# Sliding-window attention scores on six PSUM banks at a time, two of them shared by two row tiles in turn

## The chip, the cores and the metric

The kernel runs on one core of one Trainium2 chip, as one launch. The metric is the device time in microseconds (us), the median over runs. TensorE (PE in the profile) does the matmuls and transposes into PSUM, used as eight banks of 512 fp32 columns; ScalarE (ACT) does exponentials and GELU, VectorE (DVE) the copies and sums, GpSimd (POOL) masks and small arithmetic, and SyncE (SP) issues the transfers.

## The reference

Two layers, each an attention block A and an MLP block B with the same weights in both layers, on x of 2048 rows by 576 columns in bf16. Cut to what matters:

```python
def _A_ref(x, wqkv, wo):
    H = 32; Dh = D // H; W = 256                       # 32 heads of 18 columns
    q, k, v = split(x @ wqkv)
    scores = jnp.einsum("bhqd,bhkd->bhqk", q, k) * (Dh ** -0.5)
    mask = (idx[:, None] - idx[None, :] >= 0) & (idx[:, None] - idx[None, :] < W)
    p = _softmax(jnp.where(mask[None, None], scores, -1e9), axis=-1)
    return einsum("bhqk,bhkd->bhqd", p, v).reshape(B, S, D) @ wo

def _B_ref(x, w1, b1, w2, b2):                         # 576 -> 4608 -> 576
    return _gelu(_layernorm(x) @ w1 + b1) @ w2 + b2

for layer in range(2):
    x = x + _A_ref(_layernorm(x), A_wqkv, A_wo)
    x = x + _B_ref(_layernorm(x), B_w1, B_b1, B_w2, B_b2)
```

A row attends to itself and the 255 rows before it. In tiles of 128 rows, a block of keys meets three blocks of queries: its own (masked on the diagonal), the next (whole), and the one after (masked on the other side).

## The kernel before

**Tiles and chunks.** The 16 row tiles of a layer form four chunks of 512 rows, so there are eight chunks over both layers (`CH`, k = 0 to 7; k = 0 and 4 begin a layer). A head has 18 columns, padded to 32, so four heads stand in the four 32-row tiles of TensorE at once; eight groups g of four heads make the 32.

**Scores.** `units_of` (line 884) cuts a chunk's blocks into three units of 384 or 512 query columns per head; a part `(so, qo, nq, col)` is key block `so` against `nq` query blocks from `qo`, put at column `col`. `scores` (line 898) does one unit of one group as one burst on TensorE: for each part four matmuls, one per row tile j, each into a bank of its own (line 909). A burst takes two pairs of banks out of `SC = (0, 2, 4)`. ScalarE then takes the exponential of each pair in one activation (line 918), and POOL sets the masked triangles to zero in SBUF (line 939). `pv` (line 944) multiplies a group's three units by V, in four column tiles, into one bank (line 956), and VectorE transposes and normalises that (lines 967 to 977).

**Order within attention.** `E` (line 992) emits the groups of a chunk: three units per group, and the `pv` of a group behind the first unit of the next. `E0` (line 980) does this for the first three groups of chunk 0. `CUTS = (0, 3, 6, 8)` splits the eight groups of a chunk into three stages, between which the MLP of the chunk before it runs.

**Everything else on TensorE.** `qkv` (line 819) makes q, k and v; behind the first two chunks and in the MLP's first product (`G_part`, line 1051, matmul at line 1076) the array is used as two 64-row tiles which swap banks between two phases, the second phase waiting on TensorE's own semaphore (`own=True`). `mm2` (line 1099) is the MLP's second product and `tail` (line 1029) the output projection; both go through `quad` (line 779), either as one full matmul (line 781) or as four quarter column tiles (line 784), so that they can stand next to `pv` in the same tile shape. Their sums take banks from `FILL = (7, 6, 5, 4)`, the output of `pv` from `OUT`, the same four; `G_part` may take all eight. VectorE adds the sums to the residual (`resid`, line 1012).

**What sets the order.** Nothing is issued in the order of the program text. `Plan.add` records tasks with costs, priorities and banks; `Plan.schedule` (line 263) replays them by those costs, picks banks, and fixes the order on every engine and queue. A task's priority has a hand-set part and a `nudge` per stage from a table (line 480). `keep_warm` (line 249) puts filler matmuls (line 683) on TensorE where the plan leaves it idle for over 0.4 us in the first 140 us. `Sched.add` (line 65) turns reads and writes into waits on semaphores.

Of the kernel before, what the change touches and what calls it, by code (L numbers as in the profile page):

```python
# [186 lines left out]
class Plan:  # L187
# [75 lines left out]
    def schedule(self):  # L263
# [156 lines left out]
        for st, t in order:  # L420
            names = lambda rs: [n for r in rs for n in ([f"pb{b}" for b in r.banks()] if isinstance(r, Bank) else [r])]
            if t.plain:
                self.S.plain(t.eng, t.fn)
            else:
                self.S.add(t.eng, t.fn, names(t.reads), names(t.writes), dma=t.dma, ring=t.ring, own=t.own)
# [11 lines left out]
def build_kernel(nc, A_x, A_wqkv, A_wo, B_x, B_w1, B_b1, B_w2, B_b2, out):  # L437
# [19 lines left out]
    PVG = [()] * 8  # L457
    PVLAG = 1
# [21 lines left out]
    PL.nudge = {"": -230.72, "b": 275.87, "ea0.0": 68.12, "ea0.2": -36.73, "ea0.p0": 25.27, "ea0.p1": 8.39, "ea0.p2": 19.16,  # L480
# [835 lines left out]
```

## Time and profile before

| | |
|---|---|
| median of 2 runs | 865.9 us (865.78 to 866.03) |
| the profiled execution, its own time | 864.13 us |
| its span, first to last instruction | 862.3 us |
| TensorE clock granted, mean | 0.998 |
| TensorE instructions (matmuls) | 11578 |
| score matmuls, line 909 | 1408 |
| exponentials, line 918 | 384, 345.1 us busy |
| GELU, line 1086 (hT) | 276, 167.4 us busy |
| masks, line 939 | 368, 282.8 us busy |

The profile is of one execution, taken by the hardware profiler. A line such as `L909 PE MATMUL ps<-qT,kT` names the line of the kernel, the engine, the operation and the tiles written and read; `x448` is how many instructions the row holds. PE is TensorE's matmuls, PEld its weight loads, which run beside them. In a timeline the columns are the start in us, the time from there to the last end, and what ran; `[0.37 <-PE ps L840]` is idle time of that engine just before, and what ended it. Several matmuls in different row or column tiles start almost together, and a matmul's record reaches beyond the time in which the next can start.

### The profile page before, as it was taken

The numbers are of one execution on the slowest core, as the hardware profiler recorded it, in microseconds if no ns is written. First come the engines' busy times: TensorE is split into PE (matmuls) and PEld (weight loads), VectorE is DVE, ScalarE is ACT, GpSimd is POOL, SyncE is SP. The second block draws the span as 40 slices with busy tenths as digits, with TensorE's granted clock in tenths as the row PEclk, the third lists the DMA queues.
The fourth block names the chain that finished last, engine by engine and source line by source line (L and its number), as shares of the span: only waits on it lengthen the run. The fifth ranks groups of instructions, "written<-read, shape, count | busy, mean of one in ns | idle before, by whom it ended". The sixth has DMA issues, their size and how long they took to land.

```text
span 862.3 us, 26990 instructions
## 1 busy us (share of the span) xinstructions
PE 848.7 (98%) x11578; PEld 520.5 (60%) x11578; DVE 392.0 (45%) x934; ACT 593.2 (69%) x741; POOL 377.9 (44%) x560
## 2 busy tenths in 40 slices
PE   8899999999999999999999999999999999999998
PEld 6556556656556565565655655656556656656656
DVE  7689424655228542384424832655224434243012
ACT  4796788768667588573875876737787589771730
POOL 4687544465135653264421863425454276222100
PEclk9999999999999999999999999999999999999999
DMA  7887435351583615957359443673536953355320
GB/s 192 197 193 142 124 125 148 109 163 44 166 181 107 163 43 166 204 93 169 90 151 218 92 139 125 116 177 98 173 112 119 289 155 105 126 166 146 120 83 28
DMA packets 181862, 119.77 MB, mean 139 GB/s; under 512 B 107440, under 2 KB 181744, under 8 KB 181744
## 3 DMA queue, kind: packets, MB, share of 16 engines
q1 hardware_dynamic: 181744, 118.05, 53.7%
q8 instruction: 91, 1.49, 0.7%
q14 instruction: 27, 0.22, 0.1%
HBM read 90.10 MB, written 2.36 MB: 107 GB/s over the span
## 4 chain that ended last, share of the span: by engine, by line
PE 87%; DMA 4%; DVE 4%; ACT 2%; issue 2%; SPq 1%; POOL 1%; POOLq 0%; DVEq 0%; ACTq 0%
PE ps L1076 31%; PE ps L781 27%; PE ps L784 9%; PE ps L840 8%; PE ps L909 6%; PE ps L956 4%; ACT pT L918 2%; DMA xnTm<-xn 2%; PE ps L800 1%; DMA xnTa<-xn 1%; DVE x_res L1019 1%; DVE xn L721 1%; DVE st_all L696 1%; SPq L633 1%; DMA wqkv<-in_A_wqkv_dram 1%
## 5 line engine op out<-in xcount | busy, mean ns | idle before, releaser
L939 POOL TENSOR_SCALAR_AFFINE_SELECT pT<-pT 128x512 bf16<-128x512 bf16 (+1 forms) x368 | 282.8, 789 | 250.1 <-ACT pT L918 244.9
L918 ACT ACTIVATE pT<-ps 128x1024 bf16<-128x1024 f32 (+1 forms) x384 | 345.1, 974 | 58.0 <-PE ps L909 57.6
L1076 PE MATMUL ps<-xnTm,w_sb 64*128 64x512 bf16 x2592 | 290.5, 376 | 0.9 <-DVE x_res L1019 0.3
L1086 ACT ACTIVATE hT<-ps,b1col 128x512 bf16<-128x512 f32 x276 | 167.4, 687 | 173.9 <-PE ps L1076 173.4
L1076 PEld LDWEIGHTS ps<-xnTm,w_sb 64*128 64x128 bf16 x2592 | 128.8, 94 | 142.5 <-issue 6.4
L781 PE MATMUL ps<-w_sb,hT 128*128 128x288 bf16 x1506 | 201.1, 287 | 0.0
L1019 DVE TENSOR_TENSOR x_res<-ps,x_res 128x288 f32<-128x288 f32 x224 | 100.0, 450 | 188.2 <-PE ps L781 162.1
L781 PEld LDWEIGHTS ps<-w_sb,hT 128*128 128x128 bf16 x1506 | 139.9, 98 | 51.5 <-issue 15.6
L840 PE MATMUL ps<-wqkv,xnTa 64*128 64x288 bf16 x1296 | 91.7, 283 | 1.6 <-DVE x_res L1019 1.1
L967 DVE STREAM_TRANSPOSE oq<-ps 128x512 f32<-128x512 f32 x64 | 45.8, 716 | 98.9 <-PE ps L956 98.0
L784 PE MATMUL ps<-w_sb,hT 128*32 128x288 bf16 x2424 | 83.7, 287 | 0.1
L861 DVE CAST qn<-ps 128x288 bf16<-128x288 f32 x120 | 49.0, 450 | 76.4 <-PE ps L840 68.8
L840 PEld LDWEIGHTS ps<-wqkv,xnTa 64*128 64x128 bf16 x1296 | 61.3, 94 | 31.4 <-issue 2.7
L784 PEld LDWEIGHTS ps<-w_sb,hT 128*32 128x32 bf16 x2424 | 62.2, 97 | 13.6 <-issue 4.2
L909 PE MATMUL ps<-qT,kT 32*128 32x384 bf16 (+2 forms) x1216 | 64.1, 276 | 2.8 <-ACT pT L918 2.3
L696 DVE BATCH_NORM_STATS2 st_all<-x_res 128x6 f32<-128x288 f32 (+1 forms) x128 | 53.4, 442 | 6.7 <-DMA x_res<-in_A_x_dram 5.8
L709 POOL TENSOR_SCALAR vtmp<-mv_all 128x1 f32<-128x1 f32 (+1 forms) x43 | 8.8, 204 | 107.7 <-DVE mv_all L700 105.3
L848 DVE CAST vA<-ps 128x288 bf16<-128x288 f32 x64 | 26.5, 450 | 63.2 <-PE ps L840 59.5
L1092 POOL TENSOR_TENSOR x_res<-x_res,b2bc 128x576 f32<-128x576 f32 x32 | 40.2, 1275 | 32.8 <-ACT hT L1086 32.8
L956 PE MATMUL ps<-pT,vA 128*20 128x384 bf16 (+2 forms) x1408 | 50.5, 276 | 0.2 <-DVE qn L861 0.2
L909 PEld LDWEIGHTS ps<-qT,kT 32*128 32x128 bf16 x1216 | 19.4, 92 | 42.8 <-issue 26.3
L781 PE MATMUL ps<-wo_sb,attT 128*128 128x288 bf16 x320 | 42.1, 287 | 0.3 <-DVE qn L861 0.3
(56 smaller groups left out, 465.1 us busy)
## 6 DMA issues: line engine op xcount, KB each, us to landing
w_sb<-in_B_w_dram SPq DMA_DIRECT2D x46, 864.0 KB, 6.0
w_sb<-in_B_w_dram SPq DMA_DIRECT2D x48, 768.0 KB, 4.7
w_sb<-in_B_w_dram SPq DMA_DIRECT2D x96, 48.0 KB, 4.4
wqkv<-in_A_wqkv_dram SPq DMA_DIRECT2D x3, 576.0 KB, 5.6
x_res<-in_A_x_dram SPq DMA_DIRECT2D x3, 576.0 KB, 5.7
wqkv<-in_B_w_dram SPq DMA_DIRECT2D x2, 864.0 KB, 6.3
out_dram<-x_res SPq DMA_DIRECT2D x12, 144.0 KB, 2.0
wo_sb<-in_A_wo_dram SPq DMA_DIRECT2D x4, 144.0 KB, 2.6
```

Of the source, the lines that this page charges most:

```text
L696: add("dve", lambda e, i=i, s=s: e.bn_stats(st_all[:, t, i, :], s[:, t, i * HB:(i + 1) * HB]), reads=res, writes=[f"st{t}_{i}"], cost=0.37 ...
L781: return e.matmul(bank(b)[:, 0:HB], lhs, rhs, start=start, stop=stop, skip_group_check=True)
L784: ins = e.matmul(bank(b)[32 * j:32 * j + 32, 0:HB], lhs[:, 32 * j:32 * j + 32], rhs, start=start, stop=stop, tile_position=(0, 32 * j), sk ...
L840: ins = e.matmul(bank(bs[o])[:, 0:HB], xnTa[r:r + 64, c, i * 128:(i + 1) * 128], wqkv[r:r + 64, c, col:col + HB], start=(c == 4), stop=(ph ...
L861: add("dve", lambda e, b=bs[o], dst=dst: e.tensor_copy(dst, heads_of(bank(b))), reads=[bs[o]], writes=[f"qn{sl}h{o}"], cost=0.375, lat=0.1 ...
L909: ins = e.matmul(two(bs[j // 2])[:, j % 2, col:col + nq * 128], k_of(T0 + so)[0][32 * j:32 * j + 32, g, :], qs[32 * j:32 * j + 32, g, qo * ...
L918: add("act", lambda e, h2=h2: e.activation(pT[:, sl, 2 * h2:2 * h2 + 2, lo:hi], two(bs[h2])[:, :, lo:hi], ACT.Exp, scale=SCALE), reads=[bs ...
L939: add("pool", lambda e, ap=ap, pat=pat, sgn=sgn, kind=kind: e.affine_select(ap, ap, pattern=pat, compare_op=(ALU.is_ge if kind == "d" else ...
L956: ins = e.matmul(bank(bo)[32 * j:32 * j + VW, qo * 128:(qo + nq) * 128], vA[:, (T0 + so) % VS, 8 * j + g, :], pT[:, sl, j, col:col + nq * ...
L1019: add("dve", lambda e: e.tensor_tensor(x_res[:, t, sl], bank(b)[:, 0:HB], x_old[:, t, sl], ALU.add), reads=[b] + ([f"xin{t}"] if first els ...
L1076: ins = e.matmul(bank(bks[i])[:, 0:n], w1_sb[r:r + 64, sls[i], col:col + 128], xnTm[r:r + 64, k % 2, c, 0:n], start=(c == 4), stop=(ph == ...
L1086: add("act", lambda e, ff=ff, hd=hd, bk=bk: e.activation(hd[:, 0:n], bank(bk)[:, 0:n], ACT.Gelu_apprx_tanh, bias=b1col[:, ff:ff + 1]), rea ...
```

## The change

Behind the first three groups of chunk 0, `scores` is replaced by `scores3`. The third unit of a group is split into two halves of 256 columns, one per remaining unit, and each half is done in the same burst as that unit. The unit itself ("big", 384 and 128 columns) uses two pairs of banks as before. The half ("small") uses a third pair: row tiles 0 and 1 share its first bank, 2 and 3 the second, 256 columns each. The burst has three steps, so that the two tiles of a bank write it one behind the other: tiles 1 and 3 do the small part; all four tiles do the big part, in the order 0, 2, 1, 3; tiles 0 and 2 do the small part, behind a wait for the first step on TensorE's own semaphore. ScalarE takes three activations per burst (two of the big part, one of 128x4x256 of the small one). At the beginning of a layer the third unit is one small part, and the second burst of the group has four banks and no small part. Pairs come from `SC3 = (0, 2, 4, 6)`. A group then has two bursts in place of three; its `pv` stands behind the first burst of the next group. The masks are the same, from a function of their own (`masks`). The whole table of nudges is replaced, so the order on all engines and queues is another one.

Counted in the order of the two programs: bursts of scores 192 before (144 of 512 columns, 48 of 384) and 131 after (96 of six banks with 768 columns per tile, 13 of six banks with 640, 13 of 512, 9 of 384); runs of one tile shape on TensorE 416 and 308; filler matmuls 34 and 57; matmuls in all 11578 and 12024, as 141 full ones became four quarter tiles each.

```diff
@@ Plan.schedule
+            elif isinstance(t.fn, list):
+                for fn, writes, own in t.fn:
+                    self.S.add(t.eng, fn, names(t.reads), names(writes), own=own)
@@ build_kernel
-    PL.nudge = {"": -230.72, "b": 275.87, "ea0.0": 68.12, "ea0.2": -36.73, "ea0.p0": 25.27, "ea0.p1": 8.39, "ea0.p2": 19.16,
...
     SC = (0, 2, 4)
+    SC3 = (0, 2, 4, 6)
+    SCO3 = 0.38
...
+    def scores3(k, g, big, small, sl, s2, hf, prio):
...
+        bs = [Bank(SC3, True) for _ in range(3 if small else 2)]
+
+        def one(e, j, p):
+            so, qo, nq, col = p
+            if p in small:
+                out = two(bs[2])[:, j // 2, j % 2 * 256:j % 2 * 256 + nq * 128]
             else:
+                out = two(bs[j // 2])[:, j % 2, col:col + nq * 128]
+            return e.matmul(out, k_of(T0 + so)[0][32 * j:32 * j + 32, g, :], qs[32 * j:32 * j + 32, g, qo * 128:(qo + nq) * 128],
+                            start=True, stop=True, tile_position=(32 * j, 0))
...
+        if small:
+            steps = [(some([(1, small[0]), (3, small[0])]), bs[2:], False),
+                     (some([(j, p) for p in big for j in (0, 2, 1, 3)]), bs[:2], False),
+                     (some([(0, small[0]), (2, small[0])]), bs[2:], True)]
+            add("pe", steps, reads=rd, writes=bs, cost=SCO3, prio=prio, lat=0.15, alloc=bs, fifo="pa", mode="r", after=old)
...
+        if small:
+            c = small[0][3]
+            add("act", lambda e: e.activation(pT[:, s2, :, c:c + 256], two(bs[2]).rearrange("p a (b n) -> p (a b) n", b=2),
+                                              ACT.Exp, scale=SCALE),
+                reads=[bs[2]], writes=[f"p{s2}h{hf}"], cost=0.07 + 1024 * 0.00083, lat=0.17, fifo="act", prio=prio)
+            masks(s2, small, [f"p{s2}h{hf}"], hf, prio)
...
     def E(k, gs, prio):
-        us = units_of(k)
...
+        if CH[k][1]:
+            us = [[(0, 0, 3, 0), (-2, 0, 1, 384)], [(1, 1, 3, 128), (3, 3, 1, 0)], [(-1, 0, 2, 0), (2, 2, 2, 256)]]
+            halves = ((0, us[2][:1]), (1, us[2][1:]))
+        else:
+            us = [[(0, 0, 3, 0)], [(1, 1, 3, 128), (3, 3, 1, 0)], [(2, 2, 2, 256)]]
+            halves = ((0, us[2]), (1, []))
+        pend = None
         for g in gs:
...
+            sl = [slots.popleft() for _ in range(3)]
+            for n, small in halves:
                 PL.part = f".{g}"
...
+                scores3(k, g, us[n], small, sl[n], sl[2], n, prio)
+                if n == 0 and pend:
+                    pv(k, *pend, True, True, prio - 0.1)
+            pend = (g, list(zip(us, sl)), Bank(OUT))
+        pv(k, *pend, True, True, prio - 0.1)
```

More of the change, by code (lines that the diff above doesn't have):

```diff
@@ L456, in build_kernel @@
     PS = 6
-    PVG = [()] * 8
-    PVLAG = 1
     NB1 = 3
@@ L479, in build_kernel @@
     PL.turn = {"hc": 0.3, "rh": 0.05, "rc": 0.05, "ch": 0.3}
-    PL.nudge = {"": -230.72, "b": 275.87, "ea0.0": 68.12, "ea0.2": -36.73, "ea0.p0": 25.27, "ea0.p1": 8.39, "ea0.p2": 19.16,
[70 rows of a table removed]
+    PL.nudge = {"": -93.04, "b": 2.94, "ea0.0": 40.29, "ea0.1": 4.32, "ea0.2": 21.51, "ea0.p0": -34.24, "ea0.p1": -173.62,
[71 rows of a table added]
     def sb(name, shape, dtype):
@@ L896, in build_kernel, with masks @@
     slots = deque(range(PS))
+    def masks(sl, parts, rd, m0, prio):
+        blk = {}
+        for (so, qo, nq, col) in parts:
+            for q in range(nq):
+                if qo + q == so:
+                    blk[col + q * 128] = "d"
+                elif qo + q == so + 2:
+                    blk[col + q * 128] = "o"
+        runs = []
+        for c in sorted(blk):
+            if runs and runs[-1][0] == blk[c] and runs[-1][1] + runs[-1][2] * 128 == c:
+                runs[-1][2] += 1
+            else:
+                runs.append([blk[c], c, 1])
+        for mi, (kind, col, nb) in enumerate(runs, m0):
+            sgn = 1 if kind == "d" else -1
+            pat = [[0, 4]] + ([[0, nb]] if nb > 1 else []) + [[sgn, 128]]
+            ap = pT[:, sl, :, col:col + nb * 128]
+            add("pool", lambda e, ap=ap, pat=pat, sgn=sgn, kind=kind: e.affine_select(
+                ap, ap, pattern=pat, compare_op=(ALU.is_ge if kind == "d" else ALU.is_gt), fill=0.0, base=0, channel_multiplier=-sgn),
+                reads=rd, writes=[f"p{sl}m{mi}"], cost=0.12 + 0.475 * nb, prio=prio)
     def scores(k, g, parts, prio):
@@ L921, in scores @@
                 fifo="act", prio=prio)
-        blk = {}
-        for (so, qo, nq, col) in parts:
-            for q in range(nq):
-                if qo + q == so:
-                    blk[col + q * 128] = "d"
-                elif qo + q == so + 2:
-                    blk[col + q * 128] = "o"
-        runs = []
-        for c in sorted(blk):
-            if runs and runs[-1][0] == blk[c] and runs[-1][1] + runs[-1][2] * 128 == c:
-                runs[-1][2] += 1
-            else:
-                runs.append([blk[c], c, 1])
@@ L935, in scores @@
-        for mi, (kind, col, nb) in enumerate(runs):
-            sgn = 1 if kind == "d" else -1
-            pat = [[0, 4]] + ([[0, nb]] if nb > 1 else []) + [[sgn, 128]]
-            ap = pT[:, sl, :, col:col + nb * 128]
-            add("pool", lambda e, ap=ap, pat=pat, sgn=sgn, kind=kind: e.affine_select(
-                ap, ap, pattern=pat, compare_op=(ALU.is_ge if kind == "d" else ALU.is_gt), fill=0.0, base=0, channel_multiplier=-sgn),
-                reads=[f"p{sl}h0", f"p{sl}h1"], writes=[f"p{sl}m{mi}"], cost=0.12 + 0.475 * nb, prio=prio)
@@ L942, in scores, with some, fn @@
-        return sl
+        masks(sl, parts, [f"p{sl}h0", f"p{sl}h1"], 0, prio)
+        return sl
+    def scores3(k, g, big, small, sl, s2, hf, prio):
+        l, t0, nt = CH[k]
+        T0 = l * NT + t0
+        qs, qname = q_of(k)
+        bs = [Bank(SC3, True) for _ in range(3 if small else 2)]
[3 more added lines that the diff above has]
+                out = two(bs[2])[:, j // 2, j % 2 * 256:j % 2 * 256 + nq * 128]
+            else:
+                out = two(bs[j // 2])[:, j % 2, col:col + nq * 128]
+            return e.matmul(out, k_of(T0 + so)[0][32 * j:32 * j + 32, g, :], qs[32 * j:32 * j + 32, g, qo * 128:(qo + nq) * 128],
+                            start=True, stop=True, tile_position=(32 * j, 0))
+        def some(seq):
+            def fn(e):
+                ins = None
+                for j, p in seq:
+                    ins = one(e, j, p)
+                return ins
+            return fn
+        parts = big + small
+        rd = [f"{qname}{qo + i}" for (so, qo, nq, col) in parts for i in range(nq)] + [k_of(T0 + p[0])[1] for p in parts]
+        ncol = sum(p[2] for p in big) * 128
+        old = [f"p{sl}{x}" for x in ("h0", "h1", "m0", "m1", "m2")] + ([f"p{s2}{x}" for x in ("h0", "h1", "m0", "m1", "m2")] if small and hf == 0 else [])
+        if small:
[3 more added lines that the diff above has]
+            add("pe", steps, reads=rd, writes=bs, cost=SCO3, prio=prio, lat=0.15, alloc=bs, fifo="pa", mode="r", after=old)
+        else:
+            add("pe", some([(j, p) for p in big for j in range(4)]), reads=rd, writes=bs, cost=0.01 + ncol * 0.00042, prio=prio, lat=0.15,
+                alloc=bs, fifo="pa", mode="r", after=old)
+        lo = min(p[3] for p in big)
+        hi = max(p[3] + p[2] * 128 for p in big)
+        for h2 in range(2):
+            add("act", lambda e, h2=h2: e.activation(pT[:, sl, 2 * h2:2 * h2 + 2, lo:hi], two(bs[h2])[:, :, lo:hi],
+                                                     ACT.Exp, scale=SCALE),
+                reads=[bs[h2]], writes=[f"p{sl}h{h2}"], cost=0.07 + 2 * (hi - lo) * 0.00083, lat=0.17,
+                fifo="act", prio=prio)
+        masks(sl, big, [f"p{sl}h0", f"p{sl}h1"], 0, prio)
+        if small:
+            c = small[0][3]
+            add("act", lambda e: e.activation(pT[:, s2, :, c:c + 256], two(bs[2]).rearrange("p a (b n) -> p (a b) n", b=2),
+                                              ACT.Exp, scale=SCALE),
+                reads=[bs[2]], writes=[f"p{s2}h{hf}"], cost=0.07 + 1024 * 0.00083, lat=0.17, fifo="act", prio=prio)
+            masks(s2, small, [f"p{s2}h{hf}"], hf, prio)
@@ L992, in E @@
     def E(k, gs, prio):
-        us = units_of(k)
-        cut = PVG[k]
-        pend = []
+        if CH[k][1]:
+            us = [[(0, 0, 3, 0), (-2, 0, 1, 384)], [(1, 1, 3, 128), (3, 3, 1, 0)], [(-1, 0, 2, 0), (2, 2, 2, 256)]]
+            halves = ((0, us[2][:1]), (1, us[2][1:]))
+        else:
+            us = [[(0, 0, 3, 0)], [(1, 1, 3, 128), (3, 3, 1, 0)], [(2, 2, 2, 256)]]
+            halves = ((0, us[2]), (1, []))
+        pend = None
         for g in gs:
-            units = []
-            bo = Bank(OUT)
-            for n, parts in enumerate(us):
+            sl = [slots.popleft() for _ in range(3)]
+            for n, small in halves:
                 PL.part = f".{g}"
-                units.append((parts, scores(k, g, parts, prio)))
-                while pend and pend[0][0] <= 3 * g + n - PVLAG:
-                    pv(k, *pend.pop(0)[1:], prio - 0.1)
-                if n in cut or n == len(us) - 1:
-                    done = n == len(us) - 1
-                    pend.append((3 * g + n, g, units, bo, not any(x[1] == g for x in pend) and units[0][0] is us[0], done))
-                    units = []
-        for p in pend:
-            pv(k, *p[1:], prio - 0.1)
+                scores3(k, g, us[n], small, sl[n], sl[2], n, prio)
[3 more added lines that the diff above has]
+        pv(k, *pend, True, True, prio - 0.1)
         PL.part = ""
```

141 rows, old and new, of the table add are left out of this document.

## The prediction

> **What bounds the kernel now.** I read the page first (busy times, then the chain that ended last), then the busy time by stage, then the timeline of TensorE in a stretch of attention, then the groups of instructions by shape.
>
> ```profile
> span 862.3 us, 26990 instructions
> PE 848.7 (98%) x11578; PEld 520.5 (60%) x11578; DVE 392.0 (45%) x934; ACT 593.2 (69%) x741; POOL 377.9 (44%) x560
> ...
> PE 87%; DMA 4%; DVE 4%; ACT 2%; issue 2%; SPq 1%; POOL 1%; POOLq 0%; DVEq 0%; ACTq 0%
> ```
>
> TensorE is busy for 98% of the span and is 87% of the chain; no other engine reaches 70%. By stage (columns: stretch, its length, then busy time of PE, PEld, DVE, ACT, POOL, granted clock, DMA share, GB/s):
>
> ```profile
> 0.00:60.00 60.00, 52.66 (x660) 33.95 (x660) 42.77 (x115) 44.19 (x66) 36.87 (x69) 0.97 0.82 186
> 60.00:140.00 80.00, 78.59 (x1153) 47.30 (x1154) 42.48 (x103) 64.20 (x77) 46.62 (x68) 1.00 0.54 137
> 140.00:300.00 160.00, 159.96 (x2369) 97.58 (x2369) 79.99 (x194) 112.11 (x135) 77.73 (x116) 1.00 0.54 138
> ```
>
> From 140 us on TensorE has practically no idle time. So the change is priced on TensorE's own queue: what its instructions cost, and what they newly wait for. A busy TensorE is not streaming all the time, which the timeline of its matmuls shows (start, time to the last end, matmuls):
>
> ```profile
> 304.65 3.11 PE L781 MATMUL ps<-w_sb,hT 128*128 128x288 bf16 x24
> 307.69 0.40 PE L909 MATMUL ps<-qT,kT 32*128 32x384 bf16 x8
> ...
> 313.23 1.64 PE L781 MATMUL ps<-w_sb,hT 128*128 128x288 bf16 x12
> 314.80 0.40 PE L909 MATMUL ps<-qT,kT 32*128 32x384 bf16 x8
> 315.13 1.64 PE L781 MATMUL ps<-w_sb,hT 128*128 128x288 bf16 x12
> ```
>
> From start to next start, 24 full matmuls take 3.04 us and 12 take 1.57. So 12 more cost 1.47 (0.1225 each, 0.425 ns a column) and every run has 0.10 us on top: the price of going from one tile shape to another. A burst of scores (four row tiles side by side, 384 and 128 columns each) takes 0.33, thus 0.23 without the switch; the bursts of 384 columns alone stand at 0.28 in the first chunk, thus 0.18.
>
> **The change part by part.**
>
> *Fewer switches.* Counted in the order of both programs, runs of one tile shape fall from 416 to 308. 108 x 0.10 = **-10.8 us**, all on the path, as TensorE is the path.
>
> *Bursts.* 144 bursts of 512 columns and 39 of 384 go (nine of 384 stay in the first chunk): 144 x 0.23 + 39 x 0.18 = 40.1 us. In their place stand 109 bursts on six banks and 13 of 512 columns on four. In a six-bank burst row tiles 1 and 3 first do a small part (256 columns), then all four do the big part in the order 0, 2, 1, 3, then tiles 0 and 2 do the small part in the banks of 1 and 3, behind a wait on TensorE's own semaphore. The trace before has such a wait in lines 840 and 1076, mostly met long before; here it is not:
>
> ```profile
> 82.84 1.94 ACT L918 ACTIVATE pT<-ps 128x1024 bf16<-128x1024 f32 x2 [0.74 <-PE ps L909]
> ...
> 83.48 0.48 PEld L840 LDWEIGHTS ps<-wqkv,xnTa 64*128 64x128 bf16 x10 [0.21 <-issue]
> 83.49 1.52 PE L840 MATMUL ps<-wqkv,xnTa 64*128 64x288 bf16 x18
> ...
> 84.34 0.36 PEld L840 LDWEIGHTS ps<-wqkv,xnTa 64*128 64x128 bf16 x8 [0.37 <-PE ps L840]
> ```
>
> The tenth matmul starts at 83.99 and its record lasts 0.283, to 84.28; the next weight load starts at 84.34, and its matmul with it. So what waits starts 0.06 us after the end of the record. A score matmul of 256 columns has a record of 0.278. Tiles 0 and 2 can therefore go on at 0.278 + 0.06 + 0.01 = 0.35 after the burst's start, and end their 256 columns (0.109) at 0.455. Without the wait, in the order of issue, they would start behind the second part of tiles 1 and 3, at (256 + 384) x 0.425 = 0.27, and end at 0.38. No run of before has row tiles out of step, so the price has two ends: 0.33 (768 columns, tiles independent, the wait met) and 0.53 (the big part's 0.33, then the small part behind it with a new 0.10 of draining). I take 0.455, from the nearest rows. 109 x 0.455 + 13 x 0.23 = 52.6, less 40.1: **+12.5 us**. The bursts eat what the switches save. The ends give -1.1 and +20.7.
>
> Behind the waiting instruction stands all of TensorE's queue, and ScalarE for the small part only: the two big activations are released earlier.
>
> A rule on this point: the Trainium skill, "TensorEngine Tiling (Array Packing)", Key Properties, says that different tiles can execute weight loads and matmuls in parallel and operate independently. The Trainium skill, "TensorE: Matmul & The Clock Gate", The mechanism, says that matmuls start and end strictly in program order. By the first the sum would be 871; by the second, had the wait been met, a burst would be 0.38 and the sum 876. No run here shows which holds.
>
> *The same work elsewhere.* Score and attention matmuls are the same 1408 each; activations of scores fall from 384 to 371 with as many elements, the masks on POOL and the transfers on SP's queue stay as many. 141 full matmuls become 564 in quarter tiles, and 48 of those take 1.48 us where 12 full ones take 1.47: nothing. SP's queue is put in a new order, past the same weight loads (4.7 to 6.3 us to landing); TensorE hides them by running other chunks' work, with a DMA share of 0.54, and behind 140 us it waits 1.0 us in all for transfers. If that cover went, one late load would cost up to its 6 us.
>
> *Early idle time.* Where its plan leaves TensorE idle early, the program stands fillers. Their count goes from 34 to 57. A pair of them in the trace fills 0.37 us (60.44 to 60.81), so 23 more stand for **+4.3 us**. Ends: 2.5 (their columns alone) and 8.
>
> *Banks (the new wait).* Before, a burst takes two of three pairs, so the next one starts while ScalarE empties the last. Now it takes three of four, and the fourth mostly holds sums of other matmuls. The first activation starts 0.22 us behind the end of the burst's stream (319.28 to 319.73, less 0.23), here 0.54 after the burst's start. Activations follow each other at 0.91 to 0.94 (two end after 1.94, one lasts 1.03), so the second pair is free at 0.54 + 0.92 + 1.03 + 0.05 = 2.54 and the third at 3.46 (0.05: from the end of an activation to the weight load that waits for it). I went through the new order behind 140 us and added the prices of what stands between two bursts. Most intervals are 3.5 to 4.3 us: covered. Thirteen are shorter than their banks allow. Eight reuse the same three pairs with 1.3 to 2.85 us between starts and lack 8.9 us; five reuse two and lack 3.6. The worst stand at the end of the last chunk: a burst, six full matmuls, a burst, one group of attention, a burst: 1.4 and 1.3 us where 2.54 and 3.46 are needed, 1.1 + 2.2 late. Together **+12.5 us**. The same count over the order before finds nothing behind 140 us, as the trace says. Ends: 0 (a pair comes free in time) and 25 (activations that start late behind a table load, matmuls that wait for the two banks left).
>
> Sum: 862.3 - 10.8 + 12.5 + 4.3 + 12.5 = 880.8 us of span. The profiled execution itself took 864.1, the median shown is 865.9; 865.9 + 18.5 = **884.4 us**, slower by 2.1%.
>
> **The rivals.**
>
> *Tiles run independently and the wait is met.* The burst then costs 0.33, the term is -1.1 in place of +12.5: 871 us, not slower by what a measurement tells (2%). For it: in column and row tiles of before, four matmuls start 3 to 4 ns apart. Against: those are always in step, and the rows of line 840 price the wait. It decides from a burst of 0.44 us downward (883.2). The skill's first rule above is this rival.
>
> *The pairs are free in time.* Place: the thirteen short intervals. Price 12.5, so 872 us, within 2%. For it: 82 of 95 intervals behind 140 us have room. Against: the last chunk has no other matmuls to put between.
>
> *Two banks are too few for the others.* While a burst holds six banks, the outputs of lines 781 and 956 share two. Where one holds an attention output, the other must be added by VectorE (0.45 + 0.22 us, line 1019) before the next sum. One such wait in a third of the 56 groups is 12 us: 897 us. For it: from 140 us on no slack is left. Against: VectorE is 45% busy, and where 30 full matmuls stand between bursts, each output has 1.47 us before its bank is wanted again.
>
> *Faster.* Only with both first rivals and no early idle: 865.9 - 10.8 - 1.1 = 854, within 2% still.
>
> **How the numbers follow.** My case 0.50, tiles independent 0.18, pairs free 0.12, too few banks 0.17, the gain whole 0.03. A measurement of this kernel tells about 2%: 848.6 to 883.2 is the same. My case lies on the bound and runs from 876 to 892, two thirds of it above: 0.33 + 0.17 = 0.50 slower; 0.02 faster; 0.48 the same. The range reaches from below the independent tiles to above too few banks: 869 to 899.
>
> **What would show it.** Switches: runs of 0.10 us fewer by 108. Bursts: from the first small matmul to what follows 0.55 us (0.455 + 0.10), a gap ahead of the second small part put down to TensorE itself. Banks: waits of score matmuls for activations of 12 us or more behind 140 us, the worst ahead of the last two bursts. TensorE's busy share falls below 97%. I am wrong if bursts take 0.43 us to the next start, or if those waits are under 4 us.

## The result

| | before | after |
|---|---|---|
| median of 2 runs | 865.9 us | 915.59 us (915.29 to 915.89) |
| ratio to before | | 1.0583 [1.0565, 1.0601] |
| the profiled execution, its span | 864.13, 862.3 | 915.89, 914.2 |
| TensorE clock granted, mean | 0.998 | 0.991 |

The kernel became 5.8% slower: 49.7 us, where 18.5 were forecast, and outside the range. First the head of the page and the chain of the kernel after:

```profile
span 914.2 us, 27917 instructions
PE 869.3 (95%) x12024; PEld 553.9 (61%) x12024; DVE 395.0 (43%) x934; ACT 592.5 (65%) x728; POOL 376.3 (41%) x560
...
PE 82%; DVE 4%; issue 4%; DMA 3%; ACT 3%; POOL 2%; SPq 1%; POOLq 0%; DVEq 0%; ACTq 0%
```

TensorE fell from 98% to 95% busy and from 87% to 82% of the chain. ScalarE has not become the bound: it is busy for 593 us before and 592 after. By stage, with the columns of the table before (the last stretch is the end of the program):

```profile
60.00:140.00 80.00, 74.45 (x1032) 43.11 (x1032) 40.83 (x97) 57.61 (x69) 43.61 (x61) 0.99 0.48 120
140.00:300.00 160.00, 156.25 (x2280) 103.00 (x2272) 75.80 (x184) 112.41 (x134) 71.55 (x108) 1.00 0.49 126
...
720.00:914.00 194.00, 180.26 (x1982) 113.93 (x1979) 57.68 (x132) 103.39 (x131) 54.79 (x80) 0.97 0.38 115
```

From 140 to 300 us, where TensorE was idle for 0.04 us before, it is idle for 3.75, and for 13.7 in the last 194 (before: 3.1 in the last 142). A record of a matmul reaches beyond its stream, so these shares understate the loss. I took the stalls from the trace itself: for each matmul the time from the end of the stream ahead of it (its columns at 2.4 per ns; full matmuls of 288 columns follow each other at 0.123 us, 2.34 per ns) to its own start, less 0.10 us where the tile shape changes. Behind 140 us they are **3.4 us before and 43.0 after**. Put down to what released the matmul or its weight load, the 43.0 are: VectorE 19.0 (residual sums of line 1074 6.6, q and k copies of line 865 4.8, attention's transposes of line 1023 3.6, v copies of line 852 2.8, line 1026 1.2), transfers of `xnTm` 8.2, TensorE itself in line 844 3.5, POOL's masks 2.3, GELU 2.1, exponentials 1.9, the rest, some 6, unnamed or small. By the banks that the program's instructions name, all of VectorE's but the 1.2 of line 1026 are waits for a bank that VectorE was still reading. Some 6 of them are waits of the bursts themselves (line 963), for pairs in which other sums had stood.

The idle time of TensorE's matmuls behind 140 us by what ended it (total us, times, longest):

```profile
PE ps L1131 <- DMA xnTm<-xn: 8.0, 2, 6.9
PE ps L963 <- DVE x_res L1074: 2.3, 3, 1.2
PE ps L1012 <- POOL pT L920: 2.0, 2, 1.8
PE ps L1012 <- DVE qn L865: 1.9, 3, 0.6
PE ps L963 <- DVE vA L852: 1.4, 1, 1.4
```

and of its weight loads, which wait for the banks ahead of the matmuls (lines put down to "issue" left out):

```profile
PEld ps L844 <- PE ps L844: 5.9, 16, 0.4
PEld ps L963 <- ACT pT L995: 5.3, 20, 0.5
PEld ps L963 <- DVE x_res L1074: 4.8, 10, 1.4
```

A weight load that waits 0.24 us costs nothing yet, since the tile shape changes there anyway; so the 20 waits for the third activation (line 995) come to 0.7 us of stalls in all. One wait is long, 6.9 us; the others are many, none over 1.9, with many releasers. The timeline of TensorE shows what they have in common:

```profile
333.16 0.63 PE L963 MATMUL ps<-qT,kT 32*128 32x256 bf16 x12
333.87 1.51 PE L844 MATMUL ps<-wqkv,xnTa 64*128 64x288 bf16 x18
336.03 0.83 PE L1012 MATMUL ps<-pT,vA 128*20 128x384 bf16 x24 [0.65 <-DVE vA L852]
336.80 0.63 PE L963 MATMUL ps<-qT,kT 32*128 32x256 bf16 x12
337.78 0.79 PE L844 MATMUL ps<-wqkv,xnTa 64*128 64x288 bf16 x10 [0.35 <-DVE oq L1023]
```

The bursts of this stretch take banks 0 to 3 for the big part and 6 and 7 for the small one, and the one at 333.16 holds the last pair until its third activation ends, at 336.56. Lines 844 and 1012 may use banks 4 to 7 only (`FILL`, `OUT`). So they have 4 and 5. The projection of v (line 844) needs both, one for each 64-row tile. Its second phase swaps them, and must wait for the first. The attention output behind it (line 1012) needs one of the two, and waits until VectorE has copied v out of it, 0.65 us. The next projection, behind another burst on the same six, needs both again and waits until VectorE has transposed the attention output, 0.35 us. ScalarE is late nowhere in these five lines. The weight loads show the phases of line 844 at the same place:

```profile
333.84 0.51 PEld L844 LDWEIGHTS ps<-wqkv,xnTa 64*128 64x128 bf16 x10 [0.24 <-issue]
334.72 0.36 PEld L844 LDWEIGHTS ps<-wqkv,xnTa 64*128 64x128 bf16 x8 [0.36 <-PE ps L844]
```

The long wait, 6.9 us for `xnTm`, stands at the end of the last chunk's attention:

```profile
813.73 0.83 PE L1012 MATMUL ps<-pT,vA 128*20 128x384 bf16 x24
814.50 3.34 PE L785 MATMUL ps<-w_sb,hT 128*128 128x288 bf16 x24
817.67 2.61 PE L785 MATMUL ps<-wo_sb,attT 128*128 128x288 bf16 x20
820.12 3.10 PE L785 MATMUL ps<-w_sb,hT 128*128 128x288 bf16 x24
823.06 1.39 PE L785 MATMUL ps<-wo_sb,attT 128*128 128x288 bf16 x10
824.28 6.04 PE L785 MATMUL ps<-w_sb,hT 128*128 128x288 bf16 x48
830.16 1.39 PE L785 MATMUL ps<-wo_sb,attT 128*128 128x288 bf16 x10
838.44 1.89 PE L1131 MATMUL ps<-xnTm,w_sb 64*128 64x512 bf16 x8 [6.89 <-DMA xnTm<-xn]
```

The last ten output projections come behind all other work. Then sums, norm and the transposing transfer of the last row tile run with nothing beside them. The chain that ended last has them from 831 to 838.3 us, 3.3 of it the transfer:

```profile
830.98 0.47 DVE x_res L1074
...
834.98 3.32 DMA xnTm<-xn
```

In the kernel before, the 40 projections come first, and the 96 matmuls of the second product (11.9 us) hide that tail:

```profile
763.37 0.83 PE L956 MATMUL ps<-pT,vA 128*20 128x384 bf16 x24
764.03 0.91 PE L784 MATMUL ps<-w_sb,hT 128*32 128x288 bf16 x24
764.88 6.87 PE L1076 MATMUL ps<-xnTm,w_sb 64*128 64x512 bf16 x62
771.67 5.08 PE L781 MATMUL ps<-wo_sb,attT 128*128 128x288 bf16 x40
776.58 11.92 PE L781 MATMUL ps<-w_sb,hT 128*128 128x288 bf16 x96
```

### The profile page after: what moved, and what is told of

Its sections match the earlier page's. It is cut to its first block, busy times and chain, and to the rows that moved or that the text cites. A ratio compares the mean times of both kernels' runs of the same rounds, so it can differ in the third digit from the quotient of the medians.

```text
span 914.2 us, 27917 instructions
## 1 busy us (share of the span) xinstructions
PE 869.3 (95%) x12024; PEld 553.9 (61%) x12024; DVE 395.0 (43%) x934; ACT 592.5 (65%) x728; POOL 376.3 (41%) x560
## 4 chain that ended last, share of the span: by engine, by line
PE 82%; DVE 4%; issue 4%; DMA 3%; ACT 3%; POOL 2%; SPq 1%; POOLq 0%; DVEq 0%; ACTq 0%
PE ps L1131 30%; PE ps L785 24%; PE ps L788 9%; PE ps L844 8%; PE ps L963 6%; PE ps L1012 4%; POOL pT L920 1%; DVE oq L1023 1%; DVE x_res L1074 1%; PE ps L804 1%; ACT hT L1141 1%; DMA xnTm<-xn 1%; DMA qT<-qn 1%; DMA w_sb<-in_B_w_dram 1%; ACT pT L988 1%
## 5 line engine op out<-in xcount | busy, mean ns | idle before, releaser
L988 ACT ACTIVATE pT<-ps 128x1024 bf16<-128x1024 f32 (+1 forms) x244 | 231.0, 999 | 140.8 <-PE ps L963 140.5
L1131 PEld LDWEIGHTS ps<-xnTm,w_sb 64*128 64x128 bf16 x2592 | 140.1, 94 | 143.6 <-issue 17.1
L785 PE MATMUL ps<-w_sb,hT 128*128 128x288 bf16 x1410 | 184.5, 288 | 1.1 <-DVE qn L865 0.5
L785 PEld LDWEIGHTS ps<-w_sb,hT 128*128 128x128 bf16 x1410 | 134.0, 98 | 42.5 <-issue 3.1
L995 ACT ACTIVATE pT<-ps 128x1024 bf16<-128x1024 f32 x109 | 112.3, 1031 | 0.0
L844 PE MATMUL ps<-wqkv,xnTa 64*128 64x288 bf16 x1296 | 95.9, 285 | 6.7 <-DMA xnTa<-xn 2.6
L788 PE MATMUL ps<-w_sb,hT 128*32 128x288 bf16 x2808 | 96.2, 287 | 0.4
L788 PEld LDWEIGHTS ps<-w_sb,hT 128*32 128x32 bf16 x2808 | 72.0, 97 | 15.7 <-ACT hT L1141 1.1
L963 PEld LDWEIGHTS ps<-qT,kT 32*128 32x128 bf16 x1168 | 29.3, 92 | 49.2 <-issue 18.2
L1012 PEld LDWEIGHTS ps<-pT,vA 128*20 128x20 bf16 x1408 | 29.2, 92 | 23.7 <-issue 8.4
```

The lines of the kernel that those rows point to most:

```text
L785: return e.matmul(bank(b)[:, 0:HB], lhs, rhs, start=start, stop=stop, skip_group_check=True)
L788: ins = e.matmul(bank(b)[32 * j:32 * j + 32, 0:HB], lhs[:, 32 * j:32 * j + 32], rhs, start=start, stop=stop, tile_position=(0, 32 * j), sk ...
L844: ins = e.matmul(bank(bs[o])[:, 0:HB], xnTa[r:r + 64, c, i * 128:(i + 1) * 128], wqkv[r:r + 64, c, col:col + HB], start=(c == 4), stop=(ph ...
L963: return e.matmul(out, k_of(T0 + so)[0][32 * j:32 * j + 32, g, :], qs[32 * j:32 * j + 32, g, qo * 128:(qo + nq) * 128], start=True, stop=T ...
L988: add("act", lambda e, h2=h2: e.activation(pT[:, sl, 2 * h2:2 * h2 + 2, lo:hi], two(bs[h2])[:, :, lo:hi], ACT.Exp, scale=SCALE), reads=[bs ...
L995: add("act", lambda e: e.activation(pT[:, s2, :, c:c + 256], two(bs[2]).rearrange("p a (b n) -> p (a b) n", b=2), ACT.Exp, scale=SCALE), r ...
```

## The experiments

**What is to be told apart.** The theory from the traces: a burst on six banks leaves two for everything else, and the loss is the sum of many short waits for whoever empties those two (banks). The rivals: the newly found order is simply a worse one, or ends badly (order, O); ScalarE is too slow for bursts of three activations, the prediction's own case (activations, A); the second step's wait on TensorE's own semaphore, doubled by what it delays (wait, W). The times of before on the chips of the three groups were 864.55, 863.58 and 863.74 us; ratios are to those.

**Order or structure: both tables emptied.** Four kernels. e1 is the kernel before, e2 the kernel after, each with an empty table of nudges, so that neither has a found order:

```diff
-    PL.nudge = {"": -230.72, "b": 275.87, "ea0.0": 68.12, ...}
+    PL.nudge = {}
```

> The kernel before, with the table of priorities emptied, so that the order is the planner's own. It is the base for the next three, which all have an empty table. It will be slower than 865.9 us by what the table is worth, some 30 to 60 us: about 910 us.

> The changed kernel, with the table emptied too. Theory O (the new order was merely found less well, the bursts themselves cost nothing): within 15 us of the kernel before with an empty table. Theory S (the six-bank burst itself makes TensorE wait, whatever the order): slower than it by about as much as with the tables, 40 to 55 us, so some 955 us.

Measured: e1 909.0 us (1.0516 [1.0485, 1.0546]), e2 970.05 (1.1222 [1.1161, 1.1283]). Without either table the new structure costs 61 us, more than the 40 to 55 expected of S; with both, 50. So each table is worth about as much to its kernel (44 and 54 us), and under this planner the structure carries the loss, not the table. Stalls behind 140 us go from 43.8 in e1 to 89.4 in e2, VectorE's from 3.2 to 24.0, POOL's from 0.9 to 10.3, the exponentials' from 20.0 to 25.2.

**Banks alone, in the kernel before.** e3 and e4 are e1 (old bursts, no new step, no new wait) with two banks fewer for the rest. In e3 every burst also claims a third pair and doesn't use it; it is held until the second activation:

```diff
+    SCH = (0, 2, 4, 6)
-        bs = [Bank(SC, True), Bank(SC, True)]
+        bs = [Bank(SCH, True), Bank(SCH, True), Bank(SCH, True)]
-                reads=[bs[h2]], writes=[f"p{sl}h{h2}"], ...
+                reads=[bs[h2]] + ([bs[2]] if h2 else []), writes=[f"p{sl}h{h2}"], ...
```

> The kernel before with an empty table, its bursts as they were (four banks, no wait inside), but each takes a third pair of banks out of four, unused, until its second activation has ended. Theory B (the banks that a burst takes away are what costs): slower than the base by 40 us or more, although no burst has a wait in it. Theory W (the wait inside the burst is what costs): within 15 us of the base.

In e4 bursts are as before, and the sums of other matmuls and the attention outputs have two banks in place of four:

```diff
-    FILL = (7, 6, 5, 4)
-    OUT = (7, 6, 5, 4)
+    FILL = (7, 6)
+    OUT = (7, 6)
```

> The kernel before with an empty table; scores keep their three pairs, but the sums of the projections, of the second product and of the attention output get banks 7 and 6 alone, in place of 7, 6, 5 and 4. Theory B in its narrow form (two banks are too few for the other sums, TensorE waits for VectorE to empty them): slower than the base by 40 us or more, and TensorE's waits are for VectorE. Theory A of the prediction (ScalarE, which empties the pairs of the scores, is what is waited for): within 15 us of the base, as scores have more room than before.

Measured: e3 979.87 (1.1336 [1.1255, 1.1416]), 71 us over e1; e4 985.62 (1.1402 [1.1369, 1.1435]), 77 us over e1. Taking banks away, with no new burst, activation or wait of TensorE on itself, costs more than the whole change does. The planner orders each kernel anew, and fillers rise from 48 to 109 and 80; all streams of TensorE together grow by 6 and 4 us only. The stalls behind 140 us are 96 in e3 and 107 in e4, against 43.8. The idle time of weight loads in e4 shows the same releasers as the kernel after (its lines 770 and 711 are 844 and 785 there, 791 is 865 and 949 is 1074):

```profile
PEld ps L839 <- ACT pT L848: 34.2, 53, 1.7
...
PEld ps L770 <- DVE qn L791: 22.8, 21, 1.5
PEld ps L770 <- PE ps L770: 15.9, 41, 0.6
PEld ps L711 <- DVE x_res L949: 15.6, 32, 1.1
```

VectorE's share of the stalls behind 140 us is 47.6 in e4 and 24.8 in e3, against 3.2 in e1, though VectorE is busy for the same 398 to 402 us in all three. The exponentials' share grows too, from 20.0 to 37 in e3, where the held pair comes from the bursts' own, and to 28 in e4, though scores keep their pairs there. These two kernels show that scarcity of banks is enough to make such a loss; not how the loss of the change itself divides.

**How it divides: one releaser relieved at a time.** f0 is the kernel after again, 916.79 us (1.0614 [1.0586, 1.0642]), for comparison on the same chip.

> The changed kernel once more, as the base for the next three, whose instructions stand in the same order: 915 us.

f1 drops the third step of a burst from chunk 2 on, and with it the wait; the third activation reads the columns of tiles 1 and 3 twice.

```diff
-                     (some([(0, small[0]), (2, small[0])]), bs[2:], True)]
+                     (some([(0, small[0]), (2, small[0])]), bs[2:], True)][:2 if k >= 2 else 3]
...
```

> The changed kernel, from the third chunk on without the second small step of a six-bank burst (tiles 0 and 2 don't do their small part; the activation of the small part reads the columns of tiles 1 and 3 twice). The wait inside the burst is gone with it. Left out: half of the small parts' scores. A burst should fall from 0.56 us to 0.44 to the next start. Theory W (the wait inside the burst costs the time): 88 bursts by 0.12 us, 10 us, and more where others waited for it, 15 in all. Theory B (banks): at most 10 us, and less, as TensorE then waits longer for the banks: 3 to 8.

f2 lets VectorE's residual sums and copies of q, k and v read an eighth of the columns behind the early stages; the reads of PSUM stay as many.

```diff
-            add("dve", lambda e: e.tensor_tensor(x_res[:, t, sl], bank(b)[:, 0:HB], x_old[:, t, sl], ALU.add),
+        nr = HB if first or t < 4 and PL.stage[-1] in "01" else 36
+            add("dve", lambda e: e.tensor_tensor(x_res[:, t, hh * HB:hh * HB + nr], bank(b)[:, 0:nr], x_old[:, t, hh * HB:hh * HB + nr], ALU.add),
...
-                        add("dve", lambda e, b=bs[o], dst=dst: e.tensor_copy(dst, heads_of(bank(b))),
+                        add("dve", lambda e, b=bs[o], dst=dst, nj=nj, ng=ng: e.tensor_copy(dst[:, 0:nj, 0:ng, :], heads_of(bank(b))[:, 0:nj, 0:ng, :]),
```

> The changed kernel; VectorE copies or adds 36 columns in place of 288 of each sum (residual from the MLP of chunk 0 on, q, k and v from the fourth chunk on), so that banks come free some 0.25 us earlier each and VectorE's queue is shorter. Left out: seven eighths of those sums. Theory B (TensorE waits for VectorE to empty the banks left): 10 to 20 us faster. Theory A (it waits for ScalarE to empty the scores): within 4 us.

f3 takes the exponentials from chunk 2 on over half their columns.

```diff
+            mid = (lo + hi) // 2 if k >= 2 else hi
-            ... pT[:, sl, 2 * h2:2 * h2 + 2, lo:hi], two(bs[h2])[:, :, lo:hi],
+            ... pT[:, sl, 2 * h2:2 * h2 + 2, lo:mid], two(bs[h2])[:, :, lo:mid],
+            nc_ = 128 if k >= 2 else 256
```

> The changed kernel; from the third chunk on each activation of scores covers half its columns, so that the three pairs of a burst come free about 1.3 us earlier. Left out: half of the exponentials. Theory A (the pairs of the scores are emptied too late by ScalarE): 10 to 15 us faster. Theory B (the other sums' banks, emptied by VectorE): 0 to 6 us faster.

Measured:

| | us | ratio | to f0 | stalls behind 140 us (44.2 in f0) |
|---|---|---|---|---|
| f1 | 912.5 | 1.0565 [1.0532, 1.0597] | -4.3 | 50.1 |
| f2 | 908.81 | 1.0534 [1.0488, 1.0579] | -8.0 | 36.4 |
| f3 | 913.04 | 1.0570 [1.0535, 1.0604] | -3.8 | 39.5 |

The ratios of f1 and f3 overlap that of f0, and f2's barely clears it; so each is small, and none alone accounts for the loss. W is out as the larger part: it expected 15 us of f1. Halving the exponentials from chunk 2 on, which by the prediction's own pricing would have removed most of its 12.5 us, is worth some 4. The shorter bursts of f1 take 10 us off TensorE's own work (88 bursts at 0.12), and the stalls give 6 of it back: some 3 to exponentials, 2 to the transfer at the end and 1 to VectorE. TensorE arrives earlier at what it waits for. In f2, VectorE's share of the stalls falls from 19 to 11.8 and the rest stays; its 8.0 us lie between what B (10 to 20) and A (within 4) expected. An eighth of the columns makes each wait for VectorE shorter and removes none of them, so f2 bounds the share of the banks from below only.

**The end of the attention.** g1 is the kernel after with two edits: the last attention group of the last chunk must be done ahead of part of the first product, and the four output projections of that chunk come ahead of the second product. It then ends as the kernel before does.

```diff
+                    rd = rd + (["oq"] if k == NK - 2 and hf == 2 and gi == 1 else [])
-                "t7.0": -295.03, "t7.1": -198.83, "t7.3": 31.39}
+                "t7.0": -299, "t7.1": -299, "t7.2": -299, "t7.3": -299}
```

> The changed kernel with one place of its order mended: the last group of attention stands inside the MLP's product that follows, not behind it, and the four output projections of the last chunk stand ahead of the second product's matmuls that can hide what comes after them. The trace of the changed kernel has TensorE idle for 6.9 us there (a transposed row tile lands late). Theory O for this part (that wait belongs to the order that was found, not to the bursts): 7 us faster than the changed kernel, about 909 us. Theory S (attention ends late because of the bursts, and the wait only moves): within 2 us of it.

Measured: 907.56 us (1.0505 [1.0486, 1.0524]), 9.2 less than f0 and 8.0 less than the first measurement of the kernel after. Its timeline has the 40 projections in one piece again and no wait behind them (its lines 941, 1060, 714 and 952 are 1012, 1131, 785 and 1023):

```profile
805.31 0.83 PE L941 MATMUL ps<-pT,vA 128*20 128x384 bf16 x24 [0.20 <-POOL pT L849]
806.97 7.94 PE L1060 MATMUL ps<-xnTm,w_sb 64*128 64x512 bf16 x72 [0.82 <-DVE oq L952]
814.84 5.07 PE L714 MATMUL ps<-wo_sb,attT 128*128 128x288 bf16 x40
819.75 11.92 PE L714 MATMUL ps<-w_sb,hT 128*128 128x288 bf16 x96
831.61 8.59 PE L1060 MATMUL ps<-xnTm,w_sb 64*128 64x512 bf16 x78
```

So 8 to 9 of the 50 us were order after all, at one place. The wait of 0.82 us at 806.97 is no sign of the banks: the first edit makes this part of the product read `oq`, which VectorE writes there. Its matmuls write banks 0 and 1, and the attention output stands in bank 7.

**All reliefs at once.** g2 is g1 with the edits of f1, f2 and f3 together (the third activation reads tiles 1 and 3 only):

```diff
+                return e.activation(pT[:, s2, 1:4:2, c:c + 256], two(bs[2])[:, :, 256:512], ACT.Exp, scale=SCALE)
```

> The last kernel with all three reliefs at once: no second small step from the third chunk on, VectorE on 36 of 288 columns of a sum, activations of scores on half the columns (that of the small part on tiles 1 and 3 alone). The order is that of the last kernel. Left out: parts of the scores, exponentials and sums. If each of the three was covered by the others, their sum is more than what they gave alone (4.3 + 8.0 + 3.8 = 16 us): 20 to 35 us faster than the last kernel, 875 to 890 us. If they only add up, 16 us, 893 us. What stays above 866 us is what the order itself fixes.

Measured: 890.53 us (1.0300 [1.0279, 1.0320]), 17.0 less than g1. The three alone were worth 4.3 + 8.0 + 3.8 = 16.1. They add up, so they don't hide behind one another. With VectorE's copies an eighth, ScalarE's exponentials half and no wait in the burst, the kernel is still 27 us slower than before. TensorE's stalls behind 140 us are 27.7 (before: 3.4), still spread: VectorE 12.8, POOL 5.1, TensorE itself 3.6, ScalarE 2.1. The largest left are attention's transposes (5.8, with the 0.8 of g1's own edit) and the masks (5), whose work no edit shortened. That the order, found for the longer waits, keeps the rest is an argument and not tested.

**The price of the wait in a tight order.** g4 is the kernel before in its own order with one thing added: in each burst of two parts the second part waits for the first on TensorE's own semaphore.

```diff
+        if len(parts) == 2:
+            fn = [(lambda e, f=fn, p=parts[:1]: f(e, p), False), (lambda e, f=fn, p=parts[1:]: f(e, p), True)]
```

> The kernel before, in its own order and with its own banks, with TensorE's wait for itself put into its 144 bursts of two parts: the second part waits for the first. By the rows such a burst takes 0.455 us in place of 0.23, as a six-bank burst does. If TensorE pays in full, 144 x 0.225 = 32 us slower, about 897 us; if part of it is covered by later waits, 20 to 30. Theory W (this wait is the larger part of what the change costs) needs the full price here.

Measured: 902.9 us (1.0446 [1.0430, 1.0461]), 39.2 more. The idle time of weight loads there:

```profile
PEld ps L912 <- PE ps L912: 47.1, 160, 0.3
...
PEld ps L912 <- ACT pT L923: 14.2, 47, 1.1
```

There are 160 such waits, 16 more than the 144 of the expectation: those at the beginnings of layers have two parts as well. On the matmuls each costs 0.243 us, 38.9 in all, and that is the whole difference. The expectation had 0.225 for 144 of them, 32 us. In this order, where TensorE waits 3.4 us in all behind 140 us, a stall of it is paid in full and nothing comes back. W needed that, but in the six-bank burst the same wait costs only 0.08, because the big part streams meanwhile: 9 us for 109 bursts, which stand in the price of the bursts already. f1 shows that 10 us less there bring 4.

## Why the prediction missed

**Switches: right.** Forecast -10.8. Runs of one tile shape are 308, and the median gap at the frequent changes of shape is 0.091 to 0.103 us in both traces: 108 x 0.097 = -10.5.

**Bursts: right.** Forecast 0.455 us, 0.55 with the switch. The burst at 329.56 above the timeline shown starts 0.56 before what follows it:

```profile
329.56 0.63 PE L963 MATMUL ps<-qT,kT 32*128 32x256 bf16 x12
330.12 3.11 PE L785 MATMUL ps<-w_sb,hT 128*128 128x288 bf16 x24
```

Within the burst at 333.164 the second small part starts at +0.346 us, released by TensorE itself, where 0.35 was worked out. The streams of all bursts take 54.7 us against 43.5: +11.2, forecast +12.5. The rival that the wait is met is out; its premise, that tiles run independently, was also the forecast's and held.

**Early idle time: too small.** Forecast +4.3 for 23 more fillers. Their columns cost 2.5. TensorE's stalls ahead of 140 us grow by 7.6 beside it (13.7 to 21.3): +10.1. By releaser VectorE's go from 2.9 to 5.1 and TensorE's waits for itself from 0.7 to 2.3, so banks have a part in this term too. Why the fillers leave these waits unfilled is not shown by a run.

**Banks: the step that failed.** Forecast +12.5 from thirteen intervals that were shorter than their banks allow, all of it ScalarE. I went through the order asking only when the pairs of the *bursts* come free, and of those only when ScalarE has emptied them. The stalls behind 140 us grew by 39.6 us (3.4 to 43.0). The waits for VectorE (1.8 to 19.0) and of line 844 for its own swap (0.2 to 3.5) make 20.5 of that, and the prediction's sum has nothing for either. The exponentials' share is 1.9 us, below the 4 set beforehand as the mark of being wrong (3.6 in the trace of f0, the same kernel). The places of the forecast look right at the last two bursts, 1.1 and 2.2 us late by the prediction:

```profile
768.67 0.63 PE L963 MATMUL ps<-qT,kT 32*128 32x256 bf16 x12 [1.07 <-ACT pT L988]
771.11 1.46 PE L1012 MATMUL ps<-pT,vA 128*20 128x384 bf16 x24 [1.81 <-POOL pT L920]
772.50 0.85 PE L963 MATMUL ps<-qT,kT 32*128 32x256 bf16 x12
```

The 1.07 is the wait that was priced. That 1.81 lies near 2.2 is luck: it stands ahead of the attention between the bursts, which waits there for masks, and so for data, while the matmuls of the last burst wait for no bank (0.40 us in the trace of f0).

**The rival that named it was priced at little over half.** "Two banks are too few for the others" had a chance of 0.17 and 12 us, with one wait of VectorE's per three groups; the 20.5 above are its size. Against it stood that "where 30 full matmuls stand between bursts, each output has 1.47 us before its bank is wanted again". That cover exists only where full matmuls stand there. Line 844 takes both banks at once, for 0.7 us a phase, then wants them swapped (16 waits, 3.5 us of stalls behind 140 us); the attention output follows and finds both in VectorE's hands. The prediction looked for the cover in the stretch where it is good, and not where `qkv` shares the two banks. The Trainium skill, "Perfetto Trace Analysis", Matmuls, says that independent groups of matmuls should rotate through different PSUM banks, so that emptying one overlaps the next group; the trace agrees, and prices what happens where two banks are left: 0.65 and 0.35 us between neighbours at 336 and 337.8 us.

**What the prediction had no term for.** The end of the last chunk, 6.9 us until the last transposed row tile has landed (8.2 with another of 1.2). The text wrote that a late weight load "would cost up to its 6 us" if its cover went, and put it at nothing, without looking where the last projections stand in the new order. What came late was the chain from those projections on, and no weight load. g1 gives 8 to 9 us back for that place.

Together: -10.5 + 11.2 + 10.1 + 39.6 = 50.4, against 51.9 us between the two spans. Forecast: 18.5.

**What stays open.** The loss is shown to follow from the banks in kernels with empty tables (e3, e4), and shown to be spread in the kernel after (f1 to f3, g2). How far a better order could have spread the same two banks is not settled: e1 against e2 says 61 us with no table, the pair as measured 50, and g1 8 to 9 less again, so the table recovers part, and more may be to be had. What the banks cost in the kernel after is known from its trace alone (20.5 us behind 140); no run gave that kernel more banks. None of these runs of the six-bank bursts beats the kernel before.

## What to carry to other kernels

Where one operation takes more PSUM banks for longer, go through the order for those who are left with fewer, not only for the operation itself: for each bank that remains, list who fills it, who empties it, and what stands on TensorE in between. Where TensorE had no idle time left, every new wait was paid in full (g4: 160 x 0.243 us), and 10 us of switches saved were little against two banks. Look at the very end of each dependent chain in the new order too; one block of projections behind its cover cost 8 to 9 us.

## What the runs showed of the hardware

**Row tiles run out of step.** In the burst at 333.164, tiles 1 and 3 start their small part at 0 and 3 ns and tiles 0 and 2 their big part at 6 and 10. Tiles 1 and 3 start the big part at 120, when their 256 columns have streamed (107 ns at 2.4 per ns). Tiles 0 and 2 go on to their next 128 columns at 180, while the other two are at theirs until about 280. So a tile waits for its own stream only; starts were in the order of issue in this burst. The Trainium skill, "TensorEngine Tiling (Array Packing)", Key Properties, says that tiles operate independently; the trace agrees.

**A bank shared in turn works.** Two row tiles wrote different columns of the same bank one behind the other, with a semaphore of TensorE between them; the price within the burst is 0.346 - 0.27 = 0.08 us (0.27: the 640 columns of tiles 1 and 3 that are issued ahead of it).

**The granted clock is halved for a while at some of the gaps.** Its mean is 0.998 in the kernel before, 0.991 after, and 0.965 to 0.974 in e2 to e4, where TensorE is 91 or 92% busy. In the trace after it is 0.50 from 610.7 to 614.1 us, from 771.2 to 774.6 and from 836.0 to 842.8. The first two begin where waits of 1.4 and 1.8 us end, the third within the one of 6.9. Before, there is none behind 140 us, and g1 has none where the wait of 6.9 is gone. The count of stalls above takes every column at 2.4 per ns, so it holds the slower matmuls too. Reckoned with the clock granted in each stretch, they are an estimated 5 of the 43.0 us, 7 in e1 and 14 to 16 in e2 to e4: part of what idle time costs is paid again there.
